# Column sums of the memory rows in four column tiles, with an issue order for each segment of a tile

## The chip, the core and the metric

The kernel runs on one core of a Trainium2 chip. Times are microseconds (us) on the device, from the first to the last instruction of that core. The number that counts is the median of three runs. The engines named below are PE (TensorE, the matmul array), ACT (ScalarE), DVE (VectorE), POOL (GpSimd) and SP (SyncE, which here only starts transfers).

## What is computed

Four layers run in sequence over 2048 tokens of width 512: a recurrent attention layer A, a linear attention layer B, and both again with the same weights. Layer A is the long one. It cuts the tokens into 64 segments of 32, and each segment is computed together with 8 memory rows that are the output of the segment before:

```python
for s in range(n_seg):
    h = concatenate([mem, xs])                 # 8 + 32 rows
    q, k, v = h @ Wq, h @ Wk, h @ Wv           # 32 heads of 128
    p = softmax(where(mask, q @ k.T * scale, -1e9))
    o = (p @ v) @ Wo
    mem = o[:8]                                # goes into the next segment
    outs.append(o[8:])
```

The memory rows see every key, and the segment's own rows see the memory and, causally, their segment. What this case is about is one detail of the softmax: the sum of the exponentials over the keys, for the queries that are memory rows.

## The kernel before

**Steps and tiles.** One segment is one step; four segments make a tile of 128 tokens. Layer norm, the transposes of x and the projections of the last 8 tokens of each segment (the names `left...`) are done for a tile at a time (`prepare`, issued from the third segment of a tile on). The linear layer's work for a finished tile (`b_in`, and in the second half `b_out`, which also ends the kernel) is issued from the first segment of a later tile. So the four segments of a tile have different loads beside the same recurrent chain.

**The chain of a step.** Key and query projections (L793), their transposes (L815, or a transposing transfer on SP), scores of memory and tokens (L936 and L942), exponentials on ACT (L953), masks on DVE (L963, which writes the two halves of `Pm`), the sums over keys on PE (L969), their logarithm and reciprocal on ACT (L972 and L974), the product with the values on PE (L979 and L982), the division on DVE (L986), the output projection (L1084) and the selection of the new memory rows (L1109). The last of these feeds the key projection of the next step. The heads are handled in two halves, b = 0 and b = 1, so there are two sums a step. Beside this chain, with no place in it, run the attention of the tokens (`x_attention`: sums at L1014 and L1018, products L1050 and L1054), `prepare`, `b_in` and `b_out`.

**Two shapes on PE.** Most matmuls run as four column tiles of 32 columns, each writing its own 32 partitions of a PSUM bank (`tile_position=(0, 32*j)`; mode `col` below, 128*32 in the profile). The others use the array at its full width (mode `full`, 128*128). The two full-width groups on the chain are the sums and the products with the values. The sums multiply a matrix of ones with `Pm`, so each of the 128 output partitions holds the same sum.

**What sets the order.** A planner (`_Prog.schedule`) puts the program's instructions into one fixed order for each engine before the launch, by estimated durations (`c_pe`, `c_pe4`, `c_act`, `c_dve`). On the chip each engine then runs its list in that order and waits at semaphores. Among ready instructions it takes the one of highest priority, and priority is minus a due time: `step * PERIOD + OFFSET[name][k]`, where the name is the stage (`k0`, `mem1`, `x`) and k is the instruction's number in it. The names end in F for first steps, L for last ones, and nothing for all the others. On PE there are two more rules. While the mode stays the same a ready instruction of the current mode is preferred to one of the other mode, unless its priority is more than `MODE_SLACK` lower; and PE leaves its turn empty where an instruction with a priority more than 1 us better becomes ready within `LOOK`. An instruction that changes the mode is charged 0.1 us (`PE_SWITCH`).

```python
elif nd.prio < pick.prio - MODE_SLACK:
    kept.append(item)
    break
elif nd.mode == self.pe_mode:
    kept.append(held)
    pick = nd
    break
```

Of the kernel before, what the change touches and what calls it, by code (L numbers as in the profile page):

```python
# [16 lines left out]
HOP = 0.06  # L17
PE_SWITCH = 0.1
TURN = 1.8
MODE_SLACK = 257.520800  # L20

LOOK = 0.037900

PERIOD = 13.5
OFFSET = {
    "ld0": (0.00,),
    "ld1": (0.00,),
    "ld2": (0.00,),
    "ld3": (0.00,),
    "ld4": (0.00,),  # L30
    "startF": (-180.90,),
    "prepF": (-121.35, 60.85, -338.25, -337.90, -107.00, -87.50, -299.25, -329.00, -408.50, 3.85, -143.55),
    "left0F": (-363.40, -329.55, -494.35, -352.10, 94.85, -208.40, -136.40, -396.90, -232.20, -403.00, -128.90,
        -405.80, -148.00, -295.50),
    "left1F": (-209.80, -257.05, -186.90, -154.30, -433.85, 6.40, -172.20, -140.25, -80.85, -9.85, -9.35, -386.50,
        -138.50, 95.25),
    "leftv0F": (-372.65, -364.30, -359.05, -256.70, -165.10, -31.45, -453.65, -169.80, -349.15),
    "leftv1F": (11.05, -371.15, -43.60, -159.70, -312.30, -127.00, -348.85, -412.35, -37.50),
    "leftsF": (152.10, -203.75, -335.15, -313.60),
    "xlF": (-408.90,),  # L40
    "k0F": (-374.05, -352.95, -109.35, -38.25, -357.80, -283.65, -389.25),
    "k1F": (-384.40, -311.20, -269.15, -445.45, -358.65, -231.45, 6.45),
    "q0F": (-231.35, -263.70, -41.50, -77.50, -422.45, -255.85, -244.15),
    "q1F": (-403.90, -236.15, -154.40, -217.85, -201.95, 40.05, -395.10),
    "v0F": (-150.70, -57.40, -88.00, -91.90, -412.95),
    "v1F": (-398.50, -281.20, -428.10, -152.00, -135.45),
    "qlF": (-276.35, -262.00),
    "mem0F": (144.85, -273.95, -326.25, -10.00, -100.65, -352.15, -184.30, -65.00, -152.00, -199.90),
    "mem1F": (143.65, -361.45, -383.05, -187.15, -362.20, -392.75, -272.00, -305.00, -257.25, -132.25),
    "warm": (-58.15,),  # L50
    "outF": (-106.90, -344.50, -302.90, -95.35, -235.60, -405.55, -256.55, -367.55, -76.60, -394.15),
    "nextF": (-363.25, 27.95, -353.90),
    "xF": (-185.90, -377.55, 14.75, -293.55, -309.80, -426.90, -378.30, 31.70, -109.50, -293.25, -82.35, -367.45,
        -244.60, -240.60, -354.70, -77.85, -232.55, -363.15, -367.00, -361.35, 25.20, -367.30, 44.65),
    "k0": (-398.40, -409.05, -373.85, -369.85, 132.45, -419.80),
    "k1": (-365.35, -358.40, -356.75, -359.10, -107.85, -297.25, -150.20),
    "q0": (-362.10, -361.85, -360.10, -360.10, -210.50, -303.20, -149.75),
    "q1": (-355.65, -305.05, -346.50, -363.20, -182.55, -219.85, -25.65),
    "v0": (-95.30, 11.05, -162.10, -296.90, -355.00),
    "v1": (-86.30, -164.30, -100.90, 16.15, -110.55),  # L60
    "ql": (-65.10, 8.65),
    "mem0": (-95.60, -319.85, -382.80, -364.30, -364.60, -238.25, -382.75, -409.25, -242.75, -363.50),
    "mem1": (-383.00, -337.30, -215.20, -155.05, -146.75, -237.10, -384.30, 73.95, -107.50, -247.10),
    "out": (-133.90, -320.25, -243.80, -151.90, -140.55, -192.85, -130.00, -224.85, -109.70, -359.70),
    "next": (-146.50, -384.40, -71.35),
    "res": (-183.00, 64.70, -297.70, -251.95, -411.00, -412.55, -365.55, -304.60, -304.65, -295.30, -246.05,
        -110.55, -74.25, -19.80, -371.90),
    "x": (-109.05, -31.75, 114.50, -203.10, -411.65, -359.40, -250.75, -429.60, -384.75, -272.75, -52.30, -225.80,
        -224.30, -229.40, -102.00, -5.70, 33.60, -84.35, -151.60, -296.60, -389.35, -9.55, -276.50),
    "prep": (-19.30, -365.40, -305.25, -166.00, -378.25, -251.70, -384.90, -194.75, -380.20, -282.75, 77.85),  # L70
    "left0": (32.80, -324.50, -411.15, -307.75, -358.90, -202.25, -79.65, -207.35, -187.55, -161.70, -154.90,
        -304.30, -258.10),
    "left1": (-122.95, -119.30, -37.50, -257.65, 25.80, 45.20, -304.15, -368.35, -295.60, -220.55, -372.95,
        -155.60, -281.60),
    "leftv0": (-150.60, -87.70, -74.05, -89.65, 87.70, -306.35, -427.50, 74.20),
    "leftv1": (-93.05, -335.75, -148.00, -153.60, -355.55, -48.40, 175.80, -359.40),
    "lefts": (15.65, -231.70, -259.75, -320.50),
    "xl": (-368.40,),
    "bi": (-160.30, -165.65, -384.40, -460.85, -352.00, -423.00, -276.75, -132.25, -251.60, -360.20, -121.05,
        -144.60, -284.90, -386.70, -405.60, 165.25, -301.95, -305.30, -356.70, -156.05, -73.25, -115.15, 25.75,  # L80
        37.60, -11.70, -163.20, 100.35, -134.80, -166.80, -114.00, -147.35, -398.65),
    "k0L": (-245.45, -353.50, -300.20, -334.30, -361.55, -384.65, -370.40),
    "k1L": (-342.20, -303.05, -383.70, -269.65, -361.15, -244.35, -335.50),
    "lr": (-341.45, -312.30, -306.75, -164.75, -284.05, -386.00, -357.55, -334.15, -416.50, 161.80, -67.40,
        -334.55, -56.15),
    "xL": (154.80, -139.25, -428.60, -145.30, -313.00, -200.15, -368.90, -369.95, -367.85, -432.15, -360.25, 65.65,
        -193.75, -336.60, -371.50, -220.70, -310.95, -427.55, -78.15, -373.70, -404.65),
    "outL": (-183.35, -223.20, -247.40, -365.15, -74.00, -380.60, -56.90, -223.50, -345.60, -38.20),
    "resL": (-280.85, -402.40),
    "biL": (-330.50, -308.55, -333.35, -91.15, -389.95, -228.15, -76.30, -32.45, -294.50, -121.05, -167.60,  # L90
        -377.75, -262.40, -270.20, -25.45, -14.60, -313.50, 59.95, -373.25, -319.65, -43.90, -426.45, -404.80,
        159.50, 90.55, -275.05, -114.60, -274.80, -0.20, -245.85, -186.45, -160.00),
    "bm": (-410.80, -480.25, -344.35, -394.70, -170.00, -356.70, -6.85, 40.95, -34.25, 28.70, -27.10, -86.70, 81.00),
    "boF": (-189.35, -384.50, -486.20, -152.40, -345.90, -400.30, -157.90, -333.20, -255.25, -380.60, -218.45),
    "bo": (-354.35, -361.60, -26.00, -195.25, -364.05, -132.50, 137.45, -348.35, -267.60, -258.70, -358.25),
    "ldL": (-68.35, -367.55),
    "boL": (-254.80, -187.90, -323.40, -61.20, -302.90, -321.15, -73.00, -462.70, -32.35, -155.00),
    "boZ": (-401.60, -128.20, -116.30, -62.60, -31.35, -177.45, -365.75, -28.05, -77.75, -79.45),
}


# [8 lines left out]
def c_pe4(n_mm, n):  # L110
    return n_mm / 4.0 * max(0.0335, (n / 2.4 + 3.0) * 1e-3)


def c_pe(n_mm, n):
    return n_mm * max(0.0335, (n / 2.4 + 3.0) * 1e-3)
# [390 lines left out]
def _build_kernel(nc, A_x, A_mem0, A_Wq, A_Wk, A_Wv, A_Wo, A_seg_len, B_wqkv, B_wo, out):  # L506
# [8 lines left out]
    NSEG = S // SEG  # L515
# [14 lines left out]
    def sb(name, shape, dt=BF16):  # L530
        return E(nc.sbuf_tensor(name, shape, dt))
# [8 lines left out]
    one_sb = sb("one_sb", [128, 128])  # L540
# [44 lines left out]
    Pm = av(2 * 256).rearrange("p (r a q) -> p r a q", r=2, a=2)  # L585
# [30 lines left out]
    P = _Prog(nc, banks)  # L616
    add = P.add
# [74 lines left out]
    for j in range(4):  # L692
        q = slice(32 * j, 32 * j + 32)
# [8 lines left out]
    for j in range(4):  # L702
        q = slice(32 * j, 32 * j + 32)
# [14 lines left out]
    tl = P.tile()  # L718
    add("pe", lambda t, tl=tl: t.matmul(tl.f32()[:, 0:128], A8_sb[0:8, :], A8_sb[0:8, :], start=True, stop=True), 0.06,
        reads=XV, tiles=[tl])  # L720
    evac(maskbd_sb[:, :], lambda tl=tl: tl.f32()[:, 0:128], 128, tiles=[tl], writes=["maskbd"])
    tl = P.tile()
# [49 lines left out]
    cnt = {"m": 0}  # L772
    LASTW = 400
    LATE = ("x", "k0", "k1")

    def a_layer(base, first):
        def by_dma(s):
# [2 lines left out]
        def at(s, name):  # L780

            early = s <= 0 or (name[:4] == "left" and not by_dma(s))
            P.at(base + s, name + ("F" if early else "L" if s >= NSEG or (s == NSEG - 1 and name in LATE) else ""))


        def project(W, key, blk, bkeys, b, urgent):
# [129 lines left out]
        def mem_attention(s, b):  # L916
# [11 lines left out]
            k = cnt["m"] % 2  # L928
            cnt["m"] += 1
            hhs = range(4 * b, 4 * b + 4)  # L930
            tl = P.tile()
# [16 lines left out]
            else:  # L948
                P.count += 1
            add("pe", main, c_pe4(16, 40),  # L950
                reads=[("kT", b), ("qT", b), ("qL", b)], tiles=[tl], urgent=chain, mode="col")
            nq = 192 if chain else 160
            add("act", lambda a: a.activation(PQ[:, r2, b, 0:nq], tl.f32()[:, 0:nq], ACTF.Exp, scale=SCALE), c_act(nq),  # L953
                tiles=[tl], writes=[("PQ", r2, b)], urgent=chain)
# [11 lines left out]

            def sums(pe):
                for a in range(2):
                    r = pe.matmul(tl.f32()[:, 256:384], one_sb[:, :], Pm[:, k, a, :], start=(a == 0), stop=(a == 1))  # L969
                return r  # L970
            add("pe", sums, c_pe(2, 128), reads=[("Pm", k, 0), ("Pm", k, 1), "one"], tiles=[tl], urgent=True)
            add("act", lambda a: a.activation(Rm[:, k, :], tl.f32()[:, 256:384], ACTF.Ln), c_act(128), tiles=[tl],  # L972
                writes=[("Rm", k)], urgent=True)
            add("act", lambda a: a.activation(Rm[:, k, :], Rm[:, k, :], ACTF.Exp, scale=-1.0), c_act(128, 0, 1),  # L974
                reads=[("Rm", k)], writes=[("Rm", k)], urgent=True)
# [214 lines left out]
        for s in range(NSEG):  # L1190
# [12 lines left out]
            for b in range(2):  # L1203
                at(s, "v%d" % b)
                tl = project(Wv_sb, "Wv", blk, bk, b, True)
# [213 lines left out]
```

## Time and profile before

| | before |
|---|---|
| median of 3 runs | 1762.81 us (1760.12 to 1763.62) |
| span of the profiled run | 1757.0 us |
| PE busy | 1671.6 us, 95% |
| DVE, ACT, POOL busy | 65%, 64%, 19% |
| granted TensorE clock, mean | 0.993 |

The page also has a table of 40 slices of 44 us each; PE's digit is 9 in all but the first, the 20th (7, between the two halves) and the last (7). Two cautions for reading: the ends of matmuls are modelled, so that two matmul records overlap and a busy PE isn't PE at its peak; their starts are the better measure. And what is called a step length below is the distance between the last selection matmuls (L1109) of two neighbouring steps in the trace.

### The profile page before, as it was taken

The numbers are of one execution on the slowest core, as the hardware profiler recorded it, in microseconds if no ns is written. First come the engines' busy times: TensorE is split into PE (matmuls) and PEld (weight loads), VectorE is DVE, ScalarE is ACT, GpSimd is POOL, SyncE is SP. The second block draws the span as 40 slices with busy tenths as digits, with TensorE's granted clock in tenths as the row PEclk, the third lists the DMA queues.
The fourth block names the chain that finished last, engine by engine and source line by source line (L and its number), as shares of the span: only waits on it lengthen the run. The fifth ranks groups of instructions, "written<-read, shape, count | busy, mean of one in ns | idle before, by whom it ended". The sixth has DMA issues, their size and how long they took to land.

```text
span 1757.0 us, 101000 instructions
## 1 busy us (share of the span) xinstructions
PE 1671.6 (95%) x46027; PEld 1098.7 (63%) x46027; DVE 1133.8 (65%) x3960; ACT 1130.2 (64%) x3069; POOL 329.3 (19%) x660
## 2 busy tenths in 40 slices
PE   5999999999999999999799999999999999999997
PEld 2666666666666666666466666666666666666663
DVE  2566666666666666666555666667666766666657
ACT  3666666666666666666466666666666666666665
POOL 2022221112221111222102221122221112221120
PEclk9999999999999999999999999999999999999999
DMA  9222222212222222222012222122222222222223
GB/s 378 77 37 45 46 45 43 50 39 46 45 41 46 45 47 40 47 50 39 22 25 40 47 47 54 36 52 48 42 52 48 42 45 48 47 47 48 51 68 105
DMA packets 228540, 97.47 MB, mean 55 GB/s; under 512 B 207096, under 2 KB 222256, under 8 KB 226576
## 3 DMA queue, kind: packets, MB, share of 16 engines
q1 hardware_dynamic: 204784, 58.64, 17.8%
q0 software_dynamic: 21744, 19.78, 5.1%
q10 hardware_dynamic: 1584, 12.58, 1.7%
q8 instruction: 360, 5.90, 1.4%
q14 instruction: 68, 0.56, 0.1%
HBM read 29.63 MB, written 10.49 MB: 23 GB/s over the span
## 4 chain that ended last, share of the span: by engine, by line
PE 80%; DMA 8%; DVE 5%; ACT 5%; issue 1%; POOL 1%; ACTq 0%; DVEq 0%
PE pb L793 42%; PE pb L1084 14%; PE pb L815 4%; PE pb L1050 4%; DMA arena_sb<-arena_sb 4%; PE pb L1246 3%; DMA dx_sb<-y_sb 2%; PE pb L936 2%; DVE arena_sb L623 2%; PE pb L1280 2%; PE pb L969 1%; ACT arena_sb L622 1%; DMA Wk_sb<-in_A_Wk_dram 1%; PE pb L1109 1%; PE pb L764 1%
## 5 line engine op out<-in xcount | busy, mean ns | idle before, releaser
L622 ACT ACTIVATE arena_sb<-pb 128x512 bf16<-128x512 f32 (+6 forms) x1375 | 674.3, 509 | 302.6 <-PE pb L793 223.4
L638 POOL DMA_DIRECT2D dx_sb<-y_sb x504 | 256.8, 516 | 1095.6 <-DVE y_sb L1120 485.0
L793 PE MATMUL pb<-Wk_sb,arena_sb 128*32 128x512 bf16 x5120 | 346.7, 382 | 16.5 <-DVE arena_sb L623 6.5
L793 PE MATMUL pb<-Wv_sb,arena_sb 128*32 128x512 bf16 x5120 | 354.0, 379 | 1.7 <-issue 1.6
L793 PE MATMUL pb<-Wq_sb,arena_sb 128*32 128x512 bf16 x5120 | 340.0, 381 | 0.5 <-DMA Wq_sb<-in_A_Wq_dram 0.5
L1084 PE MATMUL pb<-Wo_sb,arena_sb 128*32 128x256 bf16 x10368 | 329.5, 273 | 9.9 <-DVE arena_sb L986 8.8
L1084 PEld LDWEIGHTS pb<-Wo_sb,arena_sb 128*32 128x32 bf16 x10368 | 265.8, 97 | 42.4 <-DVE arena_sb L986 20.3
L623 DVE CAST arena_sb<-pb 128x512 bf16<-128x512 f32 (+3 forms) x459 | 232.7, 519 | 83.8 <-PE pb L793 66.0
L623 DVE COPY arena_sb<-pb 128x512 bf16<-128x512 bf16 (+2 forms) x422 | 150.5, 365 | 172.7 <-PE pb L815 156.9
L623 DVE COPY arena_sb<-arena_sb 32x256 bf16<-32x256 bf16 (+2 forms) x960 | 202.3, 211 | 72.4 <-PE pb L942 18.8
L793 PEld LDWEIGHTS pb<-Wk_sb,arena_sb 128*32 128x32 bf16 x5120 | 131.9, 97 | 122.0 <-DVE arena_sb L623 8.9
L793 PEld LDWEIGHTS pb<-Wq_sb,arena_sb 128*32 128x32 bf16 x5120 | 131.9, 97 | 116.5 <-issue 2.1
L622 ACT ACTIVATE outW_sb<-pb 128x128 fp32r<-128x128 f32 x288 | 79.8, 277 | 158.3 <-PE pb L1084 153.9
L793 PEld LDWEIGHTS pb<-Wv_sb,arena_sb 128*32 128x32 bf16 x5120 | 115.7, 95 | 48.4 <-issue 2.6
L815 PEld LDWEIGHTS pb<-id_sb,arena_sb 128*32 128x32 bf16 x6304 | 110.5, 97 | 53.6 <-DVE arena_sb L623 12.1
L953 ACT ACTIVATE arena_sb<-pb 128x192 bf16<-128x192 f32 (+1 forms) x256 | 81.6, 329 | 93.2 <-PE pb L942 47.8
L815 PE MATMUL pb<-id_sb,arena_sb 128*32 128x128 bf16 x6304 | 135.7, 219 | 0.1
L1120 DVE TENSOR_TENSOR y_sb<-pb,outW_sb 64x256 bf16<-64x256 f32 x158 | 65.8, 417 | 87.1 <-ACT outW_sb L622 84.4
L1050 PE MATMUL pb<-arena_sb 128*128 128x128 bf16 x1024 | 114.0, 220 | 5.5 <-DVE arena_sb L623 4.2
L963 DVE TENSOR_TENSOR arena_sb<-arena_sb 128x128 bf16<-128x128 bf16 x504 | 86.4, 220 | 16.8 <-ACT arena_sb L953 15.7
L1050 PEld LDWEIGHTS pb<-arena_sb 128*128 128x128 bf16 x1024 | 69.4, 97 | 40.8 <-issue 19.3
L986 DVE TENSOR_TENSOR arena_sb<-pb,arena_sb 128x128 bf16<-128x128 f32 x252 | 68.0, 286 | 25.7 <-ACT arena_sb L974 15.6
(123 smaller groups left out, 1962.5 us busy)
## 6 DMA issues: line engine op xcount, KB each, us to landing
arena_sb<-arena_sb SPq DMA_TRANSPOSE x356, 2.8
Wq_sb<-in_A_Wq_dram ACTq DMA_DIRECT2D x1, 4096.0 KB, 13.6
Wk_sb<-in_A_Wk_dram ACTq DMA_DIRECT2D x1, 4096.0 KB, 24.5
Wv_sb<-in_A_Wv_dram ACTq DMA_DIRECT2D x1, 4096.0 KB, 35.0
Wo_sb<-in_A_Wo_dram SPq DMA_DIRECT2D x4, 1024.0 KB, 11.7
xs_scratch<-x_sb POOLq DMA_DIRECT2D x32, 128.0 KB, 2.0
pq_scratch<-arena_sb POOLq DMA_DIRECT2D x32, 128.0 KB, 2.5
dx_sb<-y_sb POOLq DMA_DIRECT2D x252, 12.0 KB, 2.0
```

The costliest lines, as they stand in the source:

```text
L622: return e.activation(o() if callable(o) else o, i() if callable(i) else i, ACTF.Copy)
L623: return e.tensor_copy(o() if callable(o) else o, i() if callable(i) else i)
L638: add(eng, lambda e: e.dma_start(o, i), 0.55 if eng == "pool" else 0.4, reads=reads, writes=writes, dsem="%s%d" % (kind, k), lat=lat + (0. ...
L793: r = pe.matmul(tl.f32()[32 * j:32 * j + 32, 0:512], blk[:, c, :], W[:, c, o:o + 512], start=(c == 0), stop=(c == 3), tile_position=(0, 32 ...
L815: r = pe.transpose(tt.bf16()[32 * j:32 * j + 32, 128 * i:128 * i + 128], img[:, k, o:o + 32], id_sb[:, :], tile_position=(0, 32 * j))
L953: add("act", lambda a: a.activation(PQ[:, r2, b, 0:nq], tl.f32()[:, 0:nq], ACTF.Exp, scale=SCALE), c_act(nq), tiles=[tl], writes=[("PQ", r ...
L963: add("dve", lambda v, a=a, p_=p_, w_=w_: v.tensor_tensor(wide(Pm[:, k, a, :]), p_.unsqueeze(2).to_broadcast([128, 4, 4, 8]), w_, ALU.mult ...
L986: add("dve", lambda v: v.tensor_tensor(oTb[:, s % NO, 16 * b:16 * b + 16, 0:8], pv.f32()[:, 0:128].rearrange("p (n q) -> p n q", q=8), Rm[ ...
L1050: r = pe.matmul(o, vimg[:, r2, e], Pbx[:, hh, :, :], start=i == 0, stop=False, skip_group_check=True)
L1084: r = pe.matmul(tl.f32()[32 * j:32 * j + 32, 0:256], oT[:, 4 * hh + n, :], Wo_sb[:, 8 * n + hh, 256 * d:256 * d + 256], start=(hh == 0 and ...
L1120: add("dve", lambda v: v.tensor_tensor(y_sb[0:64, k, :], tl.f32()[0:64, 0:256], outW[64:128, w, :].bitcast(F32), ALU.add), c_dve(256), rea ...
L1246: add("pe", lambda pe, c=c: pe.matmul(dst.f32()[:, :], xlnT[:, c, :], wqkv_sb[:, c, o:o + D], start=(c == 0), stop=(c == 3)), c_pe(1, 512) ...
```

## The change

Two things are changed. The sums over keys of the memory rows are written as four column tiles, so that they no longer ask for the full-width mode; the result is the same, with the four tiles each filling 32 of the 128 partitions. And the thirteen stages of a segment that repeat are given four due times in place of one, by the segment's place in its tile (`a` to `d`), with the whole table of offsets, the period and the two PE rules set anew.

```diff
-MODE_SLACK = 257.520800
-LOOK = 0.037900
-PERIOD = 13.5
+MODE_SLACK = 3.565100
+LOOK = 0.000000
+PERIOD = 12.815
...
-    "k0": (-398.40, -409.05, -373.85, -369.85, 132.45, -419.80),
...
+    "k0b": (-61.15, -28.10, -65.25, -17.20, -6.75, 11.30),
...
+    "k0c": (-20.30, -16.10, -23.70, -14.20, 21.60, -27.90),
...
+    "k0d": (-77.00, -83.60, -62.80, -52.20, 19.95, 3.00),
...
+    "k0a": (-83.65, -89.75, -65.15, -59.80, -13.55, 40.05),
...
+    EACH = ("k0", "k1", "q0", "q1", "v0", "v1", "ql", "mem0", "mem1", "out", "next", "res", "x")
...
-            P.at(base + s, name + ("F" if early else "L" if s >= NSEG or (s == NSEG - 1 and name in LATE) else ""))
+            P.at(base + s, name + ("F" if early else "L" if s >= NSEG or (s == NSEG - 1 and name in LATE) else
+                                   "abcd"[s % 4] if name in EACH else ""))
...
             def sums(pe):
                 for a in range(2):
-                    r = pe.matmul(tl.f32()[:, 256:384], one_sb[:, :], Pm[:, k, a, :], start=(a == 0), stop=(a == 1))
+                    for j in range(4):
+                        q = slice(32 * j, 32 * j + 32)
+                        r = pe.matmul(tl.f32()[q, 256:384], one_sb[:, q], Pm[:, k, a, :], start=(a == 0), stop=(a == 1),
+                                      tile_position=(0, 32 * j))
                 return r
-            add("pe", sums, c_pe(2, 128), reads=[("Pm", k, 0), ("Pm", k, 1), "one"], tiles=[tl], urgent=True)
+            add("pe", sums, c_pe4(8, 128), reads=[("Pm", k, 0), ("Pm", k, 1), "one"], tiles=[tl], urgent=True, mode="col")
```

## The prediction

> **What bounds the kernel now.** I read four views in this order: busy time by engine, busy time by stretch, the waits in front of PE, and the order on PE inside one step.
>
> The page opens with the busy times, and the chain that ended last says the same:
>
> ```profile
> PE 1671.6 (95%) x46027; PEld 1098.7 (63%) x46027; DVE 1133.8 (65%) x3960; ACT 1130.2 (64%) x3069; POOL 329.3 (19%) x660
> ...
> PE 80%; DMA 8%; DVE 5%; ACT 5%; issue 1%; POOL 1%; ACTq 0%; DVEq 0%
> ```
>
> PE is busy 95% and carries 80% of the chain. DVE and ACT have a third of their time free. The recurrence shows little, because other PE work is put beside it. Two stretches without the ends and the middle (us from the start) say how little:
>
> ```profile
> 100.00:760.00 660.00, 643.49 (x18169) 429.17 (x18170) 435.37 (x1564) 435.39 (x1196) 123.66 (x239) 1.00 0.25 45
> 900.00:1640.00 740.00, 722.55 (x20210) 478.76 (x20211) 495.95 (x1742) 491.78 (x1351) 144.45 (x278) 1.00 0.25 46
> ```
>
> The second number is the stretch, the third PE's busy time; the clock is full (1.00). Idle on PE is 660 - 643.5 = 16.5 and 740 - 722.6 = 17.4, so 34 us of 1400. The largest waits of PE are these (total, times, longest):
>
> ```profile
> PE pb L764 <- DVE arena_sb L758: 16.8, 5, 8.8
> PE pb L1084 <- DVE arena_sb L986: 8.8, 33, 0.7
> PE pb L793 <- DVE arena_sb L623: 6.5, 19, 0.4
> PE pb L936 <- DMA arena_sb<-arena_sb: 6.4, 12, 1.2
> ```
>
> The first is few and long, a start of a layer. The second is the change's own chain: 33 output projections wait, 0.27 us each, for the division that follows the sums. So what a new order can take back is small waits on PE, and PE's own losses. For those, the timeline of PE in one step at a tile's start (start, length, work):
>
> ```profile
> 299.26 1.26 PE L793 MATMUL pb<-Wv_sb,arena_sb 128*32 128x512 bf16 x20
> 300.46 0.40 PE L969 MATMUL pb<-arena_sb,one_sb 128*128 128x128 bf16 x4
> 300.79 0.29 PE L1018 MATMUL pb<-arena_sb,bo_sb 128*32 128x256 bf16 x4
> 300.91 0.20 PE L1014 MATMUL pb<-arena_sb,bo_sb 128*32 128x64 bf16 x4
> 301.04 0.23 PE L979 MATMUL pb<-arena_sb 128*128 128x128 bf16 x1
> 301.11 0.26 PE L982 MATMUL pb<-arena_sb 128*128 128x32 bf16 x4
> 301.31 0.23 PE L979 MATMUL pb<-arena_sb 128*128 128x128 bf16 x1
> 301.38 0.25 PE L982 MATMUL pb<-arena_sb 128*128 128x32 bf16 x4
> 301.93 0.51 PE L1084 MATMUL pb<-Wo_sb,arena_sb 128*32 128x256 bf16 x12 [0.29 <-DVE arena_sb L986]
> ```
>
> The reader sees PE leave the column tiles for the four sums alone (300.46), come back for L1018 and L1014, and leave again for the products. I call one such excursion a trip. At the end stands the wait of L1084.
>
> **What a trip costs.** The matmul starts in the trace give it. Four column tiles of 512 columns start a median of 0.206 us before the next four, but 0.312 us before a full-width sum: 0.106 lost. A full-width matmul of 128 columns is followed by its like after 0.056 us, and by column tiles after 0.149: 0.093 lost. A trip costs **0.20 us**. The Trainium skill, TensorEngine Tiling (Array Packing), Key Properties, says that changing the tiling mode drains TensorE; the trace agrees, with 0.093 and 0.106 us.
>
> Counted over 114 ordinary steps, there are 1.90 trips in a step, 1.0 at a tile's third segment, 3.0 at its first in the first half of the kernel. For 126 steps: 1.90 x 126 = 239 trips, 48 us. In the whole trace 20 excursions hold sums and nothing else, 17 sums and the layer norm's transposes (L764), 13 sums and L1349. In the others the sums share a trip with the products and cost none.
>
> **The change part by part.**
>
> *The sums themselves.* Removed are 252 x 2 full-width matmuls, added 252 x 8 column-tile ones, four at a time. The old spacing is 0.056 us each, so 0.112 for a pair. For the new one the nearest row is L815, the same 128 columns in column tiles: a mean start distance of 0.014 us, so 0.056 for four and 0.112 for eight. The difference is **0**. The skill's TensorE: Matmul & The Clock Gate, Part 3, has column tiles starting about 4 ns apart and running together; the trace agrees (median 4 ns between the tiles of L793 and L815). The tiling page, Restrictions and Gotchas, says that column tiling excludes the fast weight load. In this trace 97 ns (32 columns, L1084) stand against 98 (128 columns, L969), so I see no price for one weight load; six more for each pair of matmuls could bind only if L815 didn't run at 0.056 for four with the same loads. I keep 0 to 0.05 us per sum, 0 to 13 us in all, with 0 as my value.
>
> *Trips that vanish.* 20 are certain to lose their reason; of the 30 shared with L764 or L1349, the partner must still go full width, but it can join a later trip. So 20 to 50 trips, 4 to 10 us. I take 30: **-6 us**. All of it lies on PE's own path.
>
> *The wait of L1084.* After the sum come L972, L974 and L986: 0.22 (0.44 for two), 0.31 and 0.29 us on ACT and DVE. Column sums can be issued among projections as soon as `Pm` is there, and their reciprocal is then ready when the products end. Of the 8.8 us I take half: **-4 us**. The semaphores stay the same: a sum still waits for both halves of `Pm`. Behind it on PE is whatever the order puts there; if `Pm` is late, everything on PE stands.
>
> *The new order for each segment.* The steps show what the same work can take. Their usual lengths by place in the tile, from the first segment on, are 12.4, 11.7, 12.5 and 14.1 us: 50.7 a tile or 12.68 a step. The means of the two halves are 12.75 and 12.94, together 12.85. The excess, 0.17 x 126 = 21 us, is in steps that fell out of their pattern (13.0 where 11.7 is usual, 15.5 for 14.1). One due time serves four different loads at present; with four, each can repeat its good order. I take half of this, 10 us, but 2 of them are waits of L1084 that I counted already: **-8 us**.
>
> *The two rules.* The mode slack falls from 257.5 us, some 20 steps, to 3.6 us, a quarter of a step. Before, PE changes mode practically only when nothing of the current mode is ready. Now an instruction that is over 3.6 us more urgent forces a trip. That may shorten the chain and may cost trips: 0.20 us each. Trips beyond one a step number 239 - 126 = 113, less the 30 removed: 83. The order can merge some (fuller trips) and make others. I take 10 merged: **-2 us**, with a range from -17 (all 83 merged) to +25 (one more in every step). Leaving out the look-ahead of 0.038 us is below 0.2 us a case; I take 0.
>
> *The ends.* Until 45 us the 16 DMA engines are busy 98% with the weights, so no order shortens this. The last 54 us are bound by the last segment and the output layer behind it, with names that keep one due time. I take 0, and 3 us either way.
>
> Sum: 0 - 6 - 4 - 8 - 2 + 0 = -20 us. 1762.8 - 20 = **1743 us**.
>
> **The rivals.**
>
> *A larger gain.* If all 113 trips beyond one a step go (-23 us) and two thirds of the 34 us idle (-23), the time is 1717. For it speaks that the third segment runs with one trip and 0.06 us idle already. Against it: the first segment has three trips because its products, its tokens' attention and the sums become ready at different times, and joining them delays one of them.
>
> *Nothing to measure.* The 6 us of trips are paid for elsewhere: the sum is cheaper, but the order around it is no better, and PE, 97.6% busy in the stretches, has no room. 1760 to 1766.
>
> *Slower.* With a short slack, one more trip in each step (+25), less the 6 saved: 1782. Or a fixed order drawn closer to estimated times meets the real ones: PE is in order, so a sum placed 0.15 us too early in each step stops all work behind it, 0.15 x 126 = 19 us; with two such waits a step it would eat all savings and more. For it: at present all small waits together are only 34 us, so the old order is tolerant, in that PE has a stock of other ready work at most places. Against it: the estimated PE, ACT and DVE times in the code agree with the trace (0.1 us charged for a mode change against 0.093 and 0.106), so real and planned times shouldn't drift far apart. I put this case at 1778.
>
> **How the numbers follow.** The forecast case, 1730 to 1758, has 0.47. The larger gain, around 1717, 0.2. No measurable change, 0.1. Slower, around 1778, 0.23. The likeliest gives 1743. The range must leave out no more than 0.2: half of the larger gain lies above 1715, and over half of the slower case below 1779, so 1715 to 1779; the 13 us of the unknown cost of loads fit inside it. Faster by over 0.2% (3.5 us): 0.47 + 0.2 = 0.67; same 0.1; slower 0.23.
>
> **What would show it.** In the changed trace L969 has 2016 matmuls of shape 128*32, a mean start distance near 0.014 us, and no excursion to full width holds sums. Trips per step fall from 1.90 to about 1.6. The wait of L1084 for L986 falls to half of 8.8 us, and the idle of PE in the two stretches from 34 to about 22. Step lengths repeat with a smaller spread about a mean near 12.7. The prediction is wrong if trips rise over 1.9, if L969 itself comes to wait for L963 in most steps, or if the idle of PE grows: then the fixed order, not the sums, sets the time. If the gain comes with trips unchanged, my first term is wrong though the total may hold.

## The result and the profile after

The changed kernel takes 1790.95 us (median of 4 runs, 1786.23 to 1795.83) where the kernel before takes 1763.21 in the same comparison: 1.0155 times as long, with an interval of 1.0111 to 1.0198. I had forecast 1743 us, in a range up to 1779. The change made the kernel 28 us slower.

The busy times and the chain that ended last, of the kernel after:

```profile
PE 1684.8 (94%) x47539; PEld 1100.8 (61%) x47539; DVE 1128.0 (63%) x3886; ACT 1136.2 (63%) x3143; POOL 326.1 (18%) x660
...
PE 64%; DMA 14%; DVE 12%; ACT 6%; issue 3%; POOL 0%; SPq 0%; ACTq 0%; DVEq 0%
PE pb L833 33%; PE pb L1127 11%; DMA arena_sb<-arena_sb 9%; DVE arena_sb L661 7%; PE pb L855 3%; PE pb L1289 3%; PE pb L1093 3%; ACT arena_sb L660 2%; PE pb L976 2%; PE pb L1011 2%; DMA dx_sb<-y_sb 2%; DVE arena_sb L1068 1%; DMA Wk_sb<-in_A_Wk_dram 1%; PE pb L802 1%; PE pb L1323 1%
```

PE's share of the chain went from 80% to 64%. Transfers now carry 14% (8% before) and DVE 12% (5%). Among the lines, the transfers from `arena_sb` to `arena_sb` have 9%, where they had 4%. These are the transposing transfers on SP.

The two stretches without the ends, after (stretch, then PE's busy time):

```profile
100.00:760.00 660.00, 632.53 (x18365) 418.46 (x18357) 424.97 (x1502) 423.35 (x1192) 121.54 (x238) 0.99 0.25 44
900.00:1640.00 740.00, 713.41 (x20479) 466.39 (x20475) 476.78 (x1658) 488.72 (x1354) 134.98 (x263) 1.00 0.24 44
```

PE idles for 27.5 + 26.6 = 54 us of 1400, where it was 34. Over the whole profiled runs, 36.7 us apart, PE's idle time grew by 23.5 us (85.4 to 108.9) and its busy time by 13.2. As an estimate, half of the 13.2 us is 30 more excursions to full width (priced below) and half is the granted clock: its mean fell from 0.993 to 0.990, and by the clock records 19 us of full-speed time were lost, where it was 12. The waits of PE after the change (total, times, longest):

```profile
PE pb L802 <- DVE arena_sb L796: 21.2, 5, 8.9
PE pb L976 <- DMA arena_sb<-arena_sb: 18.8, 24, 2.1
PE pb L855 <- DVE arena_sb L661: 9.4, 38, 0.6
PE pb L833 <- ACT arena_sb L660: 6.2, 18, 0.3
```

The first is the start of a layer. L976 is the score line L936 of before, L855 the transpose line L815, L661 the copies and evacuations on DVE (an evacuation copies a result out of PSUM). The wait of the output projection for the division is gone from the list. In its place the scores wait 18.8 us for a transposing transfer (6.4 before), and the transposes 9.4 us for copies on DVE. What DVE and ACT themselves wait for stands in their own lists. Before:

```profile
DVE arena_sb L623 <- DMA arena_sb<-arena_sb: 14.0, 14, 3.4
ACT arena_sb L622 <- DMA arena_sb<-arena_sb: 11.3, 16, 1.1
```

After:

```profile
DVE arena_sb L661 <- DMA arena_sb<-arena_sb: 73.3, 45, 3.1
ACT arena_sb L660 <- DMA arena_sb<-arena_sb: 1.3, 2, 0.7
```

So the two together waited 25 us before and 75 after. DVE runs its list in order, so a copy that waits for a transfer holds up the evacuations behind it, and PE waits for those. A step of 16.3 us shows the direct form. First PE after the change, then the SP queue around it:

```profile
644.43 0.60 PE L833 MATMUL pb<-Wv_sb,arena_sb 128*32 128x512 bf16 x8
644.86 0.19 PE L982 MATMUL pb<-arena_sb 128*32 128x32 bf16 x4
647.15 0.28 PE L976 MATMUL pb<-arena_sb 128*32 128x40 bf16 x16 [2.10 <-DMA arena_sb<-arena_sb]
647.26 1.46 PE L833 MATMUL pb<-Wv_sb,arena_sb 128*32 128x512 bf16 x16
```

```profile
639.04 2.60 SPq L868 DMA_TRANSPOSE arena_sb<-arena_sb  x1
641.68 2.58 SPq L846 DMA_TRANSPOSE arena_sb<-arena_sb  x2
```

L868 and the first L846 are transfers of the left rows, the second L846 (1.26 us, from 643.0) is the key transfer that the scores need. It landed 4.11 us after its issue. The planner takes 3.25 for a key transfer: 1.25 us of queue time, `TURN` of 1.8 and 0.2. That is 0.86 of the 2.10 us of wait. The rest lies before the issue: the key transfer stood behind two left transfers on SP, and the first held the queue for 2.60 us where 1.25 are planned. Value projections stand behind the scores in PE's list; they were ready and could not pass. The skill's TensorE: Matmul & The Clock Gate, Part 3, says that matmuls run strictly in order; the trace agrees, with 2.10 us of idle ahead of work that needed nothing.

The wait cost more than its own length. Just after it, the granted clock fell to half for 3.41 us (the last three numbers of the view are clock, share of the DMA engines and GB/s):

```profile
647.73:651.14 3.41, 3.41 (x45) 2.15 (x38) 1.95 (x7) 1.69 (x6) 0.00 (x0) 0.50 0.00 0
```

Half of 3.41 is 1.7 us, and 2.1 + 1.7 = 3.8 is the whole excess of this step over the 12.53 us that another third segment took, from 586.7 us on, with the same 361 matmuls.

Landings in the trace of the kernel after: the key transfers land 2.5 us (median) after their issue, but 36 of 124 later than the 3.25 planned, up to 4.5. For the left rows 3.65 is planned, and 77 of 232 are later, up to 5.1. Before, where the landing is taken as the last completion signal ahead of the next transfer on the same semaphore, 27 of the key transfers and 68 of the left ones were late; the same count gives 36 and 77 after. So the transfers land late only a little more often than they did, and the new order meets late ones far more often.

### The profile page after: what moved, and what is told of

Read it like the earlier page. It is cut to its first block, busy times and chain, and to the rows that moved or that the text cites. A ratio compares the mean times of both kernels' runs of the same rounds, so it can differ in the third digit from the quotient of the medians.

```text
span 1793.7 us, 103937 instructions
## 1 busy us (share of the span) xinstructions
PE 1684.8 (94%) x47539; PEld 1100.8 (61%) x47539; DVE 1128.0 (63%) x3886; ACT 1136.2 (63%) x3143; POOL 326.1 (18%) x660
## 4 chain that ended last, share of the span: by engine, by line
PE 64%; DMA 14%; DVE 12%; ACT 6%; issue 3%; POOL 0%; SPq 0%; ACTq 0%; DVEq 0%
PE pb L833 33%; PE pb L1127 11%; DMA arena_sb<-arena_sb 9%; DVE arena_sb L661 7%; PE pb L855 3%; PE pb L1289 3%; PE pb L1093 3%; ACT arena_sb L660 2%; PE pb L976 2%; PE pb L1011 2%; DMA dx_sb<-y_sb 2%; DVE arena_sb L1068 1%; DMA Wk_sb<-in_A_Wk_dram 1%; PE pb L802 1%; PE pb L1323 1%
## 5 line engine op out<-in xcount | busy, mean ns | idle before, releaser
L660 ACT ACTIVATE arena_sb<-pb 128x512 bf16<-128x512 f32 (+6 forms) x1430 | 682.0, 495 | 358.2 <-PE pb L833 277.4
L833 PE MATMUL pb<-Wv_sb,arena_sb 128*32 128x512 bf16 x5120 | 377.6, 379 | 2.0 <-issue 1.9
L833 PE MATMUL pb<-Wq_sb,arena_sb 128*32 128x512 bf16 x5120 | 358.4, 383 | 1.0 <-DVE arena_sb L661 0.7
L661 DVE CAST arena_sb<-pb 128x512 bf16<-128x512 f32 (+2 forms) x446 | 231.7, 523 | 134.7 <-PE pb L833 93.8
L661 DVE COPY arena_sb<-arena_sb 32x256 bf16<-32x256 bf16 (+2 forms) x961 | 201.9, 213 | 146.3 <-DMA arena_sb<-arena_sb 73.3
L661 DVE COPY arena_sb<-pb 128x512 bf16<-128x512 bf16 (+1 forms) x380 | 147.0, 396 | 108.0 <-PE pb L855 82.5
L660 ACT ACTIVATE outW_sb<-pb 128x128 fp32r<-128x128 f32 x307 | 85.1, 277 | 174.2 <-PE pb L1127 146.2
L855 PE MATMUL pb<-id_sb,arena_sb 128*32 128x128 bf16 x6304 | 142.9, 220 | 10.0 <-DVE arena_sb L661 9.4
L855 PEld LDWEIGHTS pb<-id_sb,arena_sb 128*32 128x32 bf16 x6304 | 107.5, 96 | 65.0 <-DVE arena_sb L661 17.2
L1093 PE MATMUL pb<-arena_sb 128*128 128x128 bf16 x1024 | 95.6, 221 | 5.4 <-DVE arena_sb L661 4.5
L976 PE MATMUL pb<-arena_sb 128*32 128x40 bf16 x4096 | 68.2, 180 | 19.0 <-DMA arena_sb<-arena_sb 18.8
L1093 PEld LDWEIGHTS pb<-arena_sb 128*128 128x128 bf16 x1024 | 64.3, 98 | 33.4 <-DVE arena_sb L661 18.4
## 6 DMA issues: line engine op xcount, KB each, us to landing
Wo_sb<-in_A_Wo_dram SPq DMA_DIRECT2D x4, 1024.0 KB, 11.7
```

What stands on the lines that cost most here:

```text
L660: return e.activation(o() if callable(o) else o, i() if callable(i) else i, ACTF.Copy)
L661: return e.tensor_copy(o() if callable(o) else o, i() if callable(i) else i)
L833: r = pe.matmul(tl.f32()[32 * j:32 * j + 32, 0:512], blk[:, c, :], W[:, c, o:o + 512], start=(c == 0), stop=(c == 3), tile_position=(0, 32 ...
L855: r = pe.transpose(tt.bf16()[32 * j:32 * j + 32, 128 * i:128 * i + 128], img[:, k, o:o + 32], id_sb[:, :], tile_position=(0, 32 * j))
L976: r = pe.matmul(tl.f32()[32 * j:32 * j + 32, 40 * i:40 * i + 40], kT[:, hh, j, :], qT[:, hh, j, :], start=True, stop=True, tile_position=( ...
L1093: r = pe.matmul(o, vimg[:, r2, e], Pbx[:, hh, :, :], start=i == 0, stop=False, skip_group_check=True)
```

## Experiments

Theory A: the loss comes from transposing transfers that land later than the fixed order assumes, in an order that has put their readers at the assumed landing. Theory B: it is on PE itself, through more excursions to full width (291 in the trace, 261 before; the prediction calls them trips) and a worse order. Theory C: DVE stands at the residual rows, which come by other transfers.

### Taking the transposing transfers away

Each transposing transfer becomes a small plain one, so the turned layouts of keys and left rows are left out. The same three edits go into both kernels; every instruction keeps its place, its waits and its signal:

```diff
-add("sp", lambda e: e.dma_start_transpose(dst.rearrange("p h j x -> p h (j x)"), img[:, k, :]), 1.25,
+add("sp", lambda e: e.dma_start(dst[0:16, 0, 0, :], img[0:16, k, 0:32]), 1.25,
...
-add("sp", lambda e: e.dma_start_transpose(xln.rearrange("p (i x) -> p i x", i=4), img[:, k, :]), 1.25,
+add("sp", lambda e: e.dma_start(xln[0:16, 0:32], img[0:16, k, 0:32]), 1.25,
...
-add("sp", lambda e, b=b, k=k: e.dma_start_transpose(vleft[:, r2, b], img[:, k, :]), 1.25,
+add("sp", lambda e, b=b, k=k: e.dma_start(vleft[0:16, r2, b, 0, 0:32], img[0:16, k, 0:32]), 1.25,
```

In the new order (`n_light`):

> The new kernel in its own fixed order, with each of the 356 transposing transfers on SP replaced by a plain transfer of 16 rows of 32 elements with the same waits and the same completion signal; the turned layouts of half the keys and of the left rows are left out. Theory A (the transposing transfers land later than the fixed order assumes, and the new order has put their readers right at the assumed landing): the loss goes, 1742 to 1757 us. Theory B (the loss is on PE itself: 30 more excursions to full width and a worse order): the time stays within 8 us of the changed kernel, 1780 or more. Theory C (DVE stands at the residual rows that come by other transfers): as B, 1775 or more.

Measured: 1757.71 us, 0.9958 of the kernel before (0.9941 to 0.9975). Of the changed kernel's 1790.95 us, 33 are gone.

In the old order (`o_light`):

> The kernel before in its own fixed order, with the same replacement of all 356 transposing transfers; the turned layouts are left out. Theory A: the old order had room for late landings, so it gains little, 1748 to 1760 us, and ends no faster than the new kernel with the same edit. Theory B and C: the same small gain, but then 20 us or more under the new kernel with the same edit.

Measured: 1749.05 us, 0.9903 (0.9876 to 0.9930). That is 14 us under the old kernel's 1763.34 in this comparison.

So these transfers cost 33 us in the new order and 14 in the old (35 and 17 by the ratios), and about two thirds of the 28 us of loss are theirs. The two runs alone don't say that lateness is what costs: the edit also takes away most of the traffic (the DMA engines' busy share in the two stretches falls from about 0.25 to 0.06). The moved orders below separate that. One part of A's expectation failed: the new order stays 9 us slower without them. 30 more excursions at 0.22 us (below) would be 7 us of it, but the clock records of the two runs also differ by 5 us of lost time, so what makes up the 9 us is not shown. Theory C falls as the main cause. DVE waits for the residual rows in the changed kernel and then in `n_light`:

```profile
DVE x_sb L1204 <- DMA dx_sb<-y_sb: 74.8, 32, 5.9
DVE x_sb L1204 <- DMA dx_sb<-y_sb: 72.8, 32, 5.6
```

The wait stayed, and the time came back all the same. One such wait does reach PE: near 419 us the scores stand 2.08 us behind a DVE that waits for residual rows, and in `n_light` the same place still costs 1.87 us.

Only the left rows' 232 transfers in the new order (`n_left_light`), with the first edit for the left rows alone and the other two as above:

> The new kernel in its own order, with only the 232 transposing transfers of the left rows replaced (layout left out); the 124 transfers of the key projection's first half stay. Theory A: these share the SP queue with the key transfers and delay them, and DVE waits for them in front of evacuations, so more than half of the 34 us comes back: 1750 to 1770 us. If the key transfers themselves are late without company: 1775 or more. B and C: 1783 or more.

Measured: 1765.31 us, 1.0008 (0.9994 to 1.0022). Only the 124 key transfers (`n_urgent_light`):

> The new kernel in its own order, with only the 124 transposing transfers of the keys replaced (layout left out); those of the left rows stay. Theory A: the waits of PE in front of the scores (18.8 us) go, the waits of DVE for the left rows (73 us on DVE, some 15 us of it passed on to PE) stay: 1765 to 1778 us. B and C: 1783 or more.

Measured: 1768.65 us, 1.0027 (1.0015 to 1.0039). The two gains, 26 and 22 us, add to more than the 33 us of both together, so part of the loss needs both kinds. The traces show one direction. With the left transfers made small, PE's wait for the keys falls from 18.8 to 2.2 us, though 27 of the 124 key transfers (36 with them) still land later than 3.25 us after their issue. So company explains only part of the lateness after the issue; the keys also no longer stand behind long left transfers before it, and no run separates the two. The other direction doesn't show: with the key transfers made small, 77 of the 232 left transfers are late as they were, and DVE waits 75.6 us for them. What delays the others wasn't tried.

### The form of the sums, in a fixed order

New order, sums emitted at full width (`n_wide`), planned as before that edit so that no instruction changes its place:

```diff
-                    for j in range(4):
-                        q = slice(32 * j, 32 * j + 32)
-                        r = pe.matmul(tl.f32()[q, 256:384], one_sb[:, q], Pm[:, k, a, :], start=(a == 0), stop=(a == 1),
-                                      tile_position=(0, 32 * j))
+                    r = pe.matmul(tl.f32()[:, 256:384], one_sb[:, :], Pm[:, k, a, :], start=(a == 0), stop=(a == 1))
```

> The new kernel in exactly its own order on every engine, but the 252 sums emitted as full-width matmuls, as before the change. Counted in that order, excursions of PE to full width rise from 290 to 395, since most sums stand among column tiles. If an excursion costs 0.20 us and the two forms of the sum cost the same in themselves: +21 us, 1805 to 1815. If the eight column-tile matmuls of a sum were dear in themselves (a rival for the loss: 0.1 us each sum, 25 us): no slower than the changed kernel, 1785 to 1795.

Measured: 1800.82 us, 1.0229 (1.0210 to 1.0249). Against the changed kernel's 1.0155 that is 0.7% or 13 us more (5 to 21 by the two intervals), less than the 21 expected. In this run the scores wait 8.8 us for transfers, 10 less than in the changed kernel, which may hide part of the price.

The reverse in the old order (`o_col`):

> The old kernel in exactly its own order on every engine, but the 252 sums emitted as column tiles. In that order many sums stand inside full-width stretches, so excursions rise from 260 to 385: +25 us, 1783 to 1793. If the column form of the sum is dear in itself, another 10 to 25 us on top: 1795 to 1815. My prediction had a saving of 4 to 10 us for the sums in a new order; an order that was made for full-width sums can't show it.

Measured: 1797.31 us, 1.0216 (1.0201 to 1.0231), 38 us more than before, over the 25 expected and in the range that I had given to a dear column form. The trace speaks against that reading. It shows 386 excursions for 261. In it, 145 sums stand alone between two full-width matmuls. There the next full-width start comes 0.386 us after the last one (median), where two sums inside the full-width run take 3 x 0.056 = 0.168: 0.218 for the excursion. 145 x 0.218 = 32 us, less 4 for the 20 excursions that held sums alone and vanish: 28 of the 38. The clock records have another 7 us of lost time more than before. Taken whole, this run gives 38 / 125 = 0.30 us an excursion, the one before it 13 / 105 = 0.12, both together 0.22; the 0.218 of the trace is the surer number. In the changed kernel itself a sum among column tiles is over after 0.112 us (median), as it was at full width. So I see no cost of the column form in itself. It loses in the old order, where it splits full-width runs, and gains in the new one.

### Moving instructions in the fixed order

After planning, the list of instructions is put into a stored other order; table, rules and instructions stay:

```diff
     P.schedule()
+    moved = np.frombuffer(zlib.decompress(base64.b64decode(MOVED)), dtype=np.int16)
+    P.committed = [P.committed[i + int(m)] for i, m in enumerate(moved)]
```

The new kernel, moved for late landings (`n_moved`):

> The new kernel with the same instructions, table and rules, but after planning some instructions are moved to other places in their engine's fixed order (1059 of 8726 on PE, 384 of 3886 on DVE, 320 on ACT, 70 of 387 on SP). The moves were chosen so that the order loses least when the transfers land as late as they did in the trace of the changed kernel. Excursions to full width fall from 290 to 271. Theory A (late landings met by an order without room): about 27 us of the loss go, 1758 to 1770. Theory B (excursions and PE's own order): 19 excursions less, 4 us, 1783 to 1791.

Measured: 1757.91 us, 0.9982 (0.9974 to 0.9990): some 30 us faster than the changed kernel by the two ratios, and a little faster than the kernel before. The control, moved for landings as planned (`n_moved_plan`):

> A control for the run before: the same procedure, but with every transfer landing when the planner assumes it. 95 moves, excursions again 271. Theory A: the order is better on paper and no more tolerant, so it gains little, 1782 to 1792. Theory B: as much gain as in the run before, or more.

Measured: 1785.35 us, 1.0134 (1.0117 to 1.0151). Both have 271 planned excursions (272 in their traces) and the same work, and they are 27 us apart. That sets the tolerance of late landings apart from excursions. The waits of PE in `n_moved` (L1051 and L1057 are the score lines, L1097 the first product with the values), then DVE's wait for the transfers:

```profile
PE pb L1097 <- DVE arena_sb L736: 4.3, 15, 0.3
PE pb L908 <- DMA Wk_sb<-in_A_Wk_dram: 4.3, 1, 4.3
PE pb L1057 <- DVE arena_sb L736: 4.1, 5, 2.2
PE pb L1467 <- DMA arena_sb<-pq_scratch: 3.4, 5, 1.0
PE pb L1051 <- DMA arena_sb<-arena_sb: 3.0, 7, 0.9
...
DVE arena_sb L736 <- DMA arena_sb<-arena_sb: 4.9, 9, 1.2
```

and in `n_moved_plan` (L985 the scores, L864 the transposes; then DVE's wait for the transfers):

```profile
PE pb L864 <- DVE arena_sb L670: 15.1, 43, 1.4
PE pb L985 <- DMA arena_sb<-arena_sb: 11.4, 19, 1.6
...
DVE arena_sb L670 <- DMA arena_sb<-arena_sb: 82.0, 44, 3.9
```

The scores wait 3.0 us for transfers in the first and 11.4 in the control. The transposes have left the part of the first list that is shown, and wait 15.1 us in the control behind a DVE that waits 82.0 us for transfers, where `n_moved` has 4.9. The transfers themselves didn't get punctual: counted as above, 31 key and 81 left transfers are late in `n_moved`, 36 and 77 in the changed kernel. What changed is who waits for them. The control has far fewer moves (95 in all, against 1059 on PE alone), so it shows that moving for planned landings gains little, not what as many moves of another kind would do.

Last, the old kernel moved for late landings (`o_moved`):

> The old kernel with its own instructions moved by the first procedure (late landings as measured); excursions 252 for 260. Theory A: the old order loses 14 us to these transfers (o_light), so up to 14 us can come back: 1746 to 1757. Theory B: 2 us for the 8 excursions, 1758 to 1764.

Measured: 1752.95 us, 0.9946 (0.9932 to 0.9959). This is the fastest version with nothing left out: the old order, too, gained when it was moved to make room for late transfers. Eight excursions fewer are about 2 of its 8 us.

## Why the prediction was wrong

**The step that failed** is the one that gave -8 us to the new order: "with four, each can repeat its good order". I argued that "real and planned times shouldn't drift far apart" because the PE, ACT and DVE times in the code agree with the trace. Those do. I left out the transfers, whose landing spreads from 2.4 to 5.1 us where the plan has one number, 3.25 or 3.65. The new order doesn't repeat: over the 114 ordinary steps, the third segment's went from means of 12.64 and 12.61 us in the two halves to 13.00 and 13.25, the mean step from 12.92 to 13.20. 0.274 x 126 = 35 us is nearly the whole difference of the two profiled spans, 36.7.

The 21 us that this term was a share of were misread too. I took 11.7 us as the usual length of the second segment's step, but in the second half of the kernel 12.18 is usual there. With each half's own usual lengths the excess is about 13 us, not 21.

The warning stood in what I showed: the scores already waited 6.4 us in 12 cases for these transfers, with up to 1.2 us each. I read it as one small wait among others. It was the edge of a distribution that a tighter order would meet more often. My slower rival named a fixed order "drawn closer to estimated times" that meets the real ones, but I put the blame on a sum placed too early, and gave it 0.23.

**The trips.** I counted -6 us for 30 excursions removed and -2 for 10 merged. No excursion of the changed trace holds sums, as said. But excursions per step rose from 1.90 to 2.12, 291 in all for 261: near 7 us lost for 8 gained. The shorter mode slack comes with that, as I had bounded (+25 at worst); whether the slack or the due times made them wasn't tried, since another slack gives another order throughout. The price agrees where a trace shows it directly, 0.20 predicted and 0.218 in `o_col`; the times of whole runs scatter about it.

**The sums themselves.** 0 us predicted; 0.112 us each before and after.

**The wait of L1084.** I took half of 8.8 us; all of it went, though 2.4 us of waits for the division now stand before the products. That part of the mechanism was right, and the gain was given back: waits grew at the start of the chain, at scores and transposes.

**The idle of PE** was to fall to 22 us in the two stretches; it rose to 54. I had named that as the sign that the fixed order sets the time, and it is.

## What to carry to other kernels

An order fixed before the launch is only as good as its least certain duration: before trusting a tighter one, compare planned and measured completion for every kind of instruction, the transfers with their whole spread and not their median. An order made to fit its estimates can be slower than one with room in it, since that room absorbed late landings; judge orders with the measured landings drawn in. And a small wait in front of the bounding engine that occurs in some steps only is a distribution's tail, to be costed for the case that many more steps meet it.

## What the runs showed of the hardware

In the traces of before and after, a transposing transfer of 128 x 512 bf16 takes its SP queue 1.19 us at least and up to 2.7, and lands 2.4 to 5.1 us after its issue. The plain transfer of 16 rows that took its place lands after 1.6 to 3.5 us, with a median of 1.7 for the key transfers. The skill's DMA: Bandwidth & Descriptors, Issuing engines are not separate DMA queues, says that transfers started by different engines interleave on the same 16 DMA engines. That fits lateness that depends on company (36 late key transfers in the changed kernel, 27 without the left ones), but no run here took the other traffic away.

PE's idles of 2.08 and 2.10 us in the changed trace were each followed, within 1.2 us of their end, by 3.41 us at a granted clock of 0.50. Every idle of 2.0 us or more inside the two stretches of the traces here had such a fall near its end or within 1.2 us after it; so had one of 1.41 us in `o_light`, 1.7 us after its end, while one of 1.87 us in `n_light` had none. What decides it was not tried.
